# Strassen mixing on one Trainium2 core: operands made two slots ahead, the first sweep in fours, and u turned behind its exchange

## The chip, the cores and the metric

One Trainium2 chip, one of its cores. The metric is the device time of one launch in microseconds (us). The core's engines work side by side, each through its own instructions in program order: PE (matrix multiply; PEld is its weight load), DVE (vector), ACT (scalar, activation functions), POOL (GpSimd), and SP, which here only issues transfers between the device memory (DRAM) and the on-chip buffer. Matrix results land in banks of PSUM.

## The reference

All numbers are fp32. x is 2048 x 512; the caches hold 32 heads of 128.

```
xn  = layernorm(x)
s   = concat_h( softmax(q_h k_h^T / sqrt(128)) v_h ) @ wo      # last 512 cached keys, q = xn @ wq
z   = gelu(xn @ w_in)                                          # 2048 x 1376
z1, z2 = z[:, :688], layernorm(z[:, 688:])
g   = w_sp @ z2 + b_sp[:, None]                                # w_sp is 2048 x 2048: the "mixing"
out = x + s * silu((z1 * g) @ w_out)
```

The kernel keeps fp32 accuracy on a faster matmul type (fp32r): each operand is split into a high part (a cast, on ACT) and a low part (the operand minus its high part, on DVE or POOL, the helper at line 59), and each product is three matmuls, high by high, high by low, low by high.

## The kernel before, in words

The program runs in four stages, one after the other on PE. Attention and z1 come first, up to 1451 us; the change leaves them as they are. Then **z2**: 16 tiles of 128 rows in the order 8 to 15, 0 to 7 (`ZO`), two 344-column products each; ACT applies gelu while it reads PSUM (L775), DVE takes statistics (L776, L782), POOL makes the reciprocal root for a pair of tiles (L74, L75), DVE normalises both tiles (L788), and `z_split` (L792 on ACT, the low part on POOL) makes the operand of the first products.

Then the **mixing**, by one level of Strassen-Winograd. w_sp is cut in quarters a11, a12, a21, a22, and z2 in four quarters b11 to b22 (rows by columns). For each of 8 row blocks r (128 rows of the upper and 128 of the lower half) there are 7 products, P1 to P7. The 56 products are slots (`SLOTS`, `NS`): a sweep of P2 and P1 for all r, 16 slots, and then P6, P5, P7, P3, P4 for r = 0, r = 1 and so on; `first(r)` is the slot of P6. A slot is 24 matmuls of 128 x 344. Its weights are an operand made by `prep`: a cast on ACT (L832) and a rest on DVE (L59, 128 x 1024), for P4 on POOL. P5, P7, P6 and P3 need sums of quarters of w_sp (s1 = a21 + a22, a11 - a21, s1 - that, a12 - that), four `a_sum` instructions per row block (L820), the last of them on POOL. Their moving side is z2's quarters or the differences T1 to T4 of them (`t_diff`, L867; split at L876).

What sets the order: no planner, a table of events. `on(t, f, ...)` puts a call at slot t; `step(t)` first makes the operand of slot t + 2 and then runs the events of slot t. The main loop emits, for each slot, the products, then the eviction of the slot before, then the step. Every engine's queue is this program order; an instruction waits for its inputs and for its buffer to come free. Most buffers of the mixing are the eight 8 KB ones of `x8`: rows of w_sp, operands, s1, small blocks.

Evictions (`evict_1` for the sweep, `evict_2`) add products in DVE: U = P1 is stored to DRAM in the sweep and loaded again by `load_2` in the slot before P6 of its row block, with the first half of u and the rest of z1; P6's eviction (L995) adds U. A finished row block of u = z1 * g is turned in 32 x 32 squares on DVE (L986, 768 columns) and stored; the last stage loads it in another order, which completes its transpose.

Last the **out-projection**: 16 tiles of 17 matmuls of 128 x 512 (`project`), each with a load of turned u, s and x (`load_p`), a split (`split_u`: L1056 on ACT, L59 128 x 640 on DVE) and `finish_out` (silu on ACT, L1072; two DVE instructions, L1073, L1074; the store).

Of the kernel before, what the change touches and what calls it, by code (L numbers as in the profile page):

```python
# [17 lines left out]
P = 128  # L18
# [7 lines left out]
ZW = 352  # L26
# [14 lines left out]
def mixer_kernel(ctx: ExitStack, tc: tile.TileContext, x, wh, w_in, w_sp, b_sp, w_out, out):  # L41
# [715 lines left out]
    zp = ctx.enter_context(tc.tile_pool(name="zp", bufs=1, side="right", reuse_waits="tile"))  # L757
    bz = tuple(zp.tile([P, NT, ZW], F32R, name=f"bz_{a}") for a in "hl")
    zr_stack = ExitStack()
    zrp = zr_stack.enter_context(tc.tile_pool(name="zrp", bufs=1, side="right", reuse_waits="tile"))  # L760
    zr = zrp.tile([P, NT, 2, NB], F32, name="zr")
    p1_dram = dram.tile([P, RP, NB], F32, name="p1_dram")
    u0_dram = dram.tile([P, RP, NB], F32, name="u0_dram")
    uD = dram.tile([NT, P, NF * P], F32, name="u_dram")
# [7 lines left out]
    def z_gelu(i, n):  # L772
        if n == 2:
            zst[i] = stats.tile([P, 2, 6], F32, name="stz")
        nc.scalar.activation(zr[:, i, n - 2], zps[i, n][:, :NB], AF.Gelu_apprx_tanh)  # L775
        nc.vector.bn_stats(zst[i][:, n - 2, :], zr[:, i, n - 2])  # L776

    def z_norm(pos):
        g, j = divmod(pos, 2)
        if j == 0:  # L780
            zmv[g] = stats.tile([P, 2, 2], F32, name="mvz")
        nc.vector.bn_aggr(zmv[g][:, j, :], zst[ZO[pos]])  # L782
        if j == 1:
            r = stats.tile([P, 2], F32, name="rz_r")
            rsqrt(zmv[g][:, :, 1], r, 2, stats.tile([P, 2], F32, name="rz_t"))
            for k in range(2):
                t = zr[:, ZO[pos - 1 + k]].rearrange("p n f -> p (n f)")
                nc.vector.tensor_scalar(t, t, zmv[g][:, k, 0:1], r[:, k:k + 1], op0=OP.subtract, op1=OP.mult)  # L788

    def z_split(i, engine):  # L790
        hi, lo = (t[:, i, :NB] for t in bz)
        nc.scalar.copy(hi, zr[:, i, 0])  # L792
        rest(engine, lo, zr[:, i, 0], hi)


    SLOTS = [(r, k) for r in range(RP) for k in ("P2", "P1")] \
# [7 lines left out]
    rows, s1, ops, tt, t2, bank = {}, {}, {}, {}, {}, {}  # L804
# [5 lines left out]
    def a_blocks(r):  # L810
        HW = RP * P
        return rows["a", r][:, :HW], rows["a", r][:, HW:], rows["b", r][:, :HW], rows["b", r][:, HW:]

    def a_sum(r, k, engine):
        a11, a12, a21, a22 = a_blocks(r)
        if k == 0:
            s1[r] = x8([P, RP * P], F32)
        to, x0, x1, op = ((s1[r], a21, a22, OP.add), (a21, a11, a21, OP.subtract),
                          (a11, s1[r], a11, OP.subtract), (a12, a12, a11, OP.subtract))[k]
        engine.tensor_tensor(to, x0, x1, op=op)  # L820

    def prep(n, engine):
        r, k = SLOTS[n]
        HW = RP * P
        if k in ("P2", "P1"):
            src = rows["s", r][:, HW:] if k == "P2" else rows["s", r][:, :HW]
# [8 lines left out]
    def operand(k, c):  # L835
        if k in ("P1", "P4"):
            return tuple(t[:, c, :NB] for t in bz)
        if k in ("P2", "P3"):
            return tuple(t[:, RP + c, :NB] for t in bz)
        return tuple(t[:, c, :NB] for t in tt[k])  # L840

    def products(n):
# [3 lines left out]
        if first_of:  # L846
            bank[r, name] = pp.tile([P, 512], F32, name=name)
        ps = bank[r, name][:, :NB]
        op = ops.pop(n)
        for c in range(RP):  # L850
            rh, rl = operand(k, c)
# [5 lines left out]
    def pair(j):  # L857
        return slice(2 * j, 2 * j + 2), slice(RP + 2 * j, RP + 2 * j + 2)

    def t_diff(j, k):  # L860
        c, d = pair(j)
        b11, b12, b21, b22 = zr[:, c, 0], zr[:, c, 1], zr[:, d, 0], zr[:, d, 1]
        if k == "T2":
            t2[j] = t2_tile[:, j % 2, :, :NB]
        to, x0, x1 = {"T1": (b11, b12, b11), "T3": (b12, b22, b12), "T2": (t2.get(j), b22, b11),
                      "T4": (b21, b21, t2.get(j))}[k]
        nc.vector.tensor_tensor(to, x0, x1, op=OP.subtract)  # L867

    def t_split_z(j, k, engine):
        c, d = pair(j)  # L870
        src = {"T2": t2.get(j), "T1": zr[:, c, 0], "T3": zr[:, c, 1], "B22": zr[:, d, 1], "T4": zr[:, d, 0]}[k]
        if k in ("B22", "T4"):
            hi, lo = (t[:, d if k == "B22" else c, :NB] for t in bz)
        else:
            hi, lo = (t[:, c, :NB] for t in tt[{"T2": "P6", "T1": "P5", "T3": "P7"}[k]])
# [9 lines left out]
    for r in range(RP):  # L885
        on(2 * r - 6 if r else -8, load_rows, ("s", r), r)
        on(first(r) - 7, load_rows, ("b", r), r + RP)
        on(first(r) - 6, load_rows, ("a", r), r)
        for k, (d, e) in enumerate(((-4, V), (-3, V), (-3, V), (-2, G))):
            on(first(r) + d, a_sum, r, k, e)  # L890
    for j in range(4):
        on(-4 + 2 * j, t_diff, j, "T1")
        on(-4 + 2 * j, t_diff, j, "T3")
        on(3 * j + 1, t_diff, j, "T2")
        on(3 * j + 1, t_split_z, j, "T2", V)
        on(3 * j + 2, t_diff, j, "T4")
        on(3 * j + 2, t_split_z, j, "T1", V)
        on(3 * j + 3, t_split_z, j, "T3", V)
        on(15, t_split_z, j, "B22", G)
        on(16, t_split_z, j, "T4", V)  # L900

    def step(t):
        if 0 <= t + 2 < NS and t + 2 > 1:
# [24 lines left out]
    M = FH - (NF - 1) * P  # L928
    pp = ctx.enter_context(tc.tile_pool(name="pp2", bufs=2, space=PSUM, reuse_waits="tile"))
    tpool = {}  # L930
    for k in ("P7", "P5", "P6"):
        tpool[k] = ExitStack() if k == "P6" else ctx
        pool = tpool[k].enter_context(tc.tile_pool(name=f"tp{k}", bufs=1, reuse_waits="tile"))
# [214 lines left out]
```

## Time and profile before

| | us |
|---|---|
| median of 3 runs (lowest to highest) | 1826.93 (1826.82 to 1831.71) |
| the profiled execution: its time, its span | 1824.3, 1822.5 |
| PE busy in the span | 1778.2 (98%) |
| DVE, ACT, POOL busy | 1516.3, 1174.9, 1287.3 |
| z2 stage, 1451.0 to 1508.4: PE busy | 56.89 of 57.4 |
| mixing, 1508.4 to 1750.6: PE busy | 66.84 of 71.6 up to 1580.0, then 152.97 of 170.6 |
| out-projection, 1750.6 to 1818.0: PE busy | 64.05 of 67.4 |

How to read it: a share over the whole span says little here, since attention fills 80% of it at a busy PE. The stages that the change touches are read one by one: how long PE was in each, how long it would take at the pace of an undisturbed stretch, and which wait ended last before each gap. In rows of a timeline the bracket at the end is the idle time of the engine before the instruction and what ended it.

### The profile page before, as it was taken

How to read it: one execution, taken by the hardware profiler on the slowest of the kernel's cores; microseconds unless marked ns; L12 is line 12 of the kernel's file. 1: busy time of each engine (PE TensorE's matmuls, PEld its weight loads, DVE VectorE, ACT ScalarE, POOL GpSimd, SP SyncE). 2: the span in 40 equal slices, each digit the busy share in tenths (PEclk: the TensorE clock that was granted, in tenths of full speed). 3: DMA queues.
4: the chain of work that ended last, by engine and by line, in shares of the span. 5: the costliest groups of instructions: out<-in, count | busy, mean ns of one | idle time of the engine just before them, and what ended most of it. 6: DMA issues, size and time to landing. Idle time of an engine off the chain costs nothing.

```text
span 1822.5 us, 28703 instructions
## 1 busy us (share of the span) xinstructions
PE 1778.2 (98%) x8460; PEld 1516.2 (83%) x8460; DVE 1516.3 (83%) x2468; ACT 1174.9 (64%) x2632; POOL 1287.3 (71%) x1203
## 2 busy tenths in 40 slices
PE   8999999999999999999999999999999999799998
PEld 7888888888888887888888888888888998798987
DVE  5689988899999888888888888888888467788865
ACT  4777777767777776677777777777776434533333
POOL 2798898898998987788888888888887241233220
PEclk9999999999999999999999999999999999999999
DMA  5688897988988989787777877877777724445488
GB/s 186 196 231 237 252 263 224 264 240 246 268 241 237 266 252 281 257 243 228 223 217 230 223 218 230 232 220 233 223 232 233 255 73 151 167 166 182 150 259 245
DMA packets 182526, 408.89 MB, mean 224 GB/s; under 512 B 24448, under 2 KB 61568, under 8 KB 162144
## 3 DMA queue, kind: packets, MB, share of 16 engines
q1 hardware_dynamic: 175456, 398.59, 73.4%
q10 hardware_dynamic: 6912, 8.46, 1.3%
q8 instruction: 66, 1.08, 0.2%
q14 instruction: 92, 0.75, 0.1%
HBM read 237.02 MB, written 169.93 MB: 223 GB/s over the span
## 4 chain that ended last, share of the span: by engine, by line
PE 74%; DVE 12%; DMA 7%; ACT 3%; issue 2%; SPq 1%; POOL 1%; ACTq 0%; DVEq 0%; POOLq 0%
PE ps_a L450 15%; PE ps L67 12%; PE ps L65 12%; PE ps L66 12%; PE ps_a L517 6%; PE ps_a L515 6%; PE ps_a L516 6%; DVE x L820 2%; DMA U<-p_dram 2%; DVE x L59 2%; PE ps_a L65 2%; PE ps_a L66 2%; PE ps_a L67 2%; DMA x<-u_dram 1%; DMA p_dram<-pL 1%
## 5 line engine op out<-in xcount | busy, mean ns | idle before, releaser
L59 POOL TENSOR_TENSOR pT_l<-pL,pT_h 128x512 fp32r<-128x512 f32 x507 | 657.4, 1300 | 186.0 <-ACT pT_h L507 181.1
L479 ACT ACTIVATE prob<-ps,nm 128x512 f32<-128x512 f32 x512 | 354.0, 691 | 340.0 <-DVE nm L477 332.3
L539 DVE SCALAR_TENSOR_TENSOR sacc<-ps,sums,sacc 128x512 f32<-128x512 f32 x496 | 369.7, 746 | 128.1 <-PE ps L67 122.5
L450 PE MATMUL ps_a<-x,x 128*128 128x512 f32 x1302 | 376.4, 389 | 4.3 <-DMA x<-x_dram 3.3
L488 DVE STREAM_TRANSPOSE pL<-prob 128x512 f32<-128x512 f32 x512 | 358.6, 700 | 2.7 <-ACT prob L479 2.7
L477 DVE TENSOR_REDUCE nm<-ps 128x1 f32<-128x512 f32 x512 | 340.0, 664 | 6.6 <-PE ps L67 6.5
L507 ACT CAST pT_h<-pL 128x512 fp32r<-128x512 f32 x512 | 318.5, 622 | 18.4 <-DMA x<-x_dram 6.7
L450 PEld LDWEIGHTS ps_a<-x,x 128*128 128x128 f32 x1302 | 244.5, 188 | 56.3 <-DMA x<-x_dram 4.1
L59 POOL TENSOR_TENSOR wl<-raw,wh 128x512 fp32r<-128x512 f32 x186 | 241.7, 1299 | 13.4 <-ACT wh L144 13.4
L517 PE MATMUL ps_a<-pT_l,wh 128*128 128x512 f32 x512 | 200.4, 391 | 1.6 <-POOL pT_l L59 1.5
L65 PE MATMUL ps<-wh,qT_h 128*128 128x512 f32 x512 | 199.9, 390 | 0.6 <-DVE sacc L539 0.6
L67 PE MATMUL ps<-wh,qT_l 128*128 128x512 f32 x512 | 199.9, 390 | 0.3
L515 PE MATMUL ps_a<-pT_h,wh 128*128 128x512 f32 x512 | 200.0, 391 | 0.0
L65 PE MATMUL ps<-wh,oT_h 128*128 128x512 f32 x512 | 199.7, 390 | 0.0
L67 PE MATMUL ps<-wh,oT_l 128*128 128x512 f32 x512 | 199.5, 390 | 0.0
L66 PE MATMUL ps<-wl,qT_h 128*128 128x512 f32 x512 | 199.5, 390 | 0.0
L516 PE MATMUL ps_a<-pT_h,wl 128*128 128x512 f32 x512 | 199.5, 390 | 0.0
L66 PE MATMUL ps<-wl,oT_h 128*128 128x512 f32 x512 | 199.4, 390 | 0.0
L59 POOL TENSOR_TENSOR x<-wq,x 128x256 fp32r<-128x256 f32 x186 | 138.5, 745 | 1.5 <-ACT x L432 1.5
L144 ACT CAST wh<-raw 128x512 fp32r<-128x512 f32 x188 | 117.9, 627 | 2.0 <-issue 1.1
L517 PEld LDWEIGHTS ps_a<-pT_l,wh 128*128 128x128 f32 x512 | 96.2, 188 | 24.4 <-POOL pT_l L59 4.7
L67 PEld LDWEIGHTS ps<-wh,qT_l 128*128 128x128 f32 x512 | 96.3, 188 | 22.0 <-DVE qT_l L59 2.0
(213 smaller groups left out, 3375.5 us busy)
## 6 DMA issues: line engine op xcount, KB each, us to landing
p_dram<-pL SPq DMA_DIRECT2D x128, 1024.0 KB, 4.8
pL<-p_dram SPq DMA_DIRECT2D x256, 192.0 KB, 4.0
raw<-wh SPq DMA_DIRECT2D x188, 256.0 KB, 6.3
pL<-p_dram SPq DMA_DIRECT2D x256, 128.0 KB, 4.0
x<-w_sp SPq DMA_DIRECT2D x24, 1024.0 KB, 5.1
pL<-p_dram SPq DMA_DIRECT2D x256, 64.0 KB, 4.0
wq<-wh SPq DMA_DIRECT2D x62, 256.0 KB, 5.6
x_dram<-rawx SPq DMA_DIRECT2D x32, 256.0 KB, 6.0
```

Source lines behind the costliest of these rows:

```text
L59: engine.tensor_tensor(lo, whole, hi.bitcast(F32), op=OP.subtract)
L65: nc.tensor.matmul(ps, lh, rh, start=first, stop=False)
L66: nc.tensor.matmul(ps, lh, rl, start=False, stop=False)
L67: nc.tensor.matmul(ps, ll, rh, start=False, stop=last)
L450: nc.tensor.matmul(qps[g, bank], wt["q", g, k][a][:, c * P:(c + 1) * P], X[g * 2 // H][ORDER[k]][:, b, c], start=first, stop=r == 5, skip_ ...
L477: nc.vector.tensor_reduce(nm, ps, axis=AX.X, op=OP.max, negate=True)
L479: nc.scalar.activation(prob[t], ps, AF.Exp, bias=nm, accum_out=sums[b][:, j:j + 1])
L488: nc.vector.transpose(pL[b][:, :, j * P:j * P + P].rearrange("p a (c q) -> p a c q", q=Q), prob.pop(t).rearrange("p (a c q) -> p a c q", a ...
L507: nc.scalar.copy(h, p)
L515: nc.tensor.matmul(pps[b], vh, ph, start=c == 0, stop=False)
L517: nc.tensor.matmul(pps[b], vh, pl, start=False, stop=c == 3)
L539: nc.vector.scalar_tensor_tensor(at, ps, rs, at, op0=OP.mult, op1=OP.add)
```

## The change

- z2 and its differences are kept in blocks of one size from one pool (`br`, 20 blocks, and `bl`, 5) instead of large fixed tiles; blocks are handed out anew as they come free. For the last eight tiles of z2 the normalisation is done by ACT (an Identity activation with scale and bias, L805), with two one-column POOL instructions per pair ahead of it (L804).
- The sweep goes P2 of r = 0 to 3, P1 of r = 0 to 3, P2 of r = 4 to 7, P1 of r = 4 to 7. Its rows of w_sp come as halves for two r at a time (`load_halves`).
- s1 has a buffer of its own; all four a_sums are on DVE; the T differences and splits have other slots; half of the last splits go to POOL.
- U of r = 0 stays on chip; for the others it is loaded four slots ahead of P6. z1 is loaded in thirds at f - 3 to f - 1, gelu at f to f + 2, and u is stored unturned in halves at f + 4 to f + 6. P5's eviction is one DVE add instead of an ACT copy; P7's eviction goes to a PSUM bank. The two-bank pools become 2, 4 and 2 banks (ps_a, ps_c, ps_f).
- In the out-projection tiles are loaded four ahead and split two ahead; `split_u` turns u after the load (two DVE transposes); the last add is on POOL; x is loaded apart from u and s. w_out, reordered on the host, is loaded at slot 43, and the first two tiles are split at the last two slots of the mixing.
- In the main loop the eviction and the step come ahead of the slot's products in program order.

```diff
+    def hilo(k, j, pool=None):
+        if pool is not None:
+            HL[k, j] = blk(pool)
+        return tuple(HL[k, j][:, a, :, :NB] for a in range(2))
...
     def z_norm(pos):
...
+                if pos < RP:
+                    nc.vector.tensor_scalar(t, t, mean, rs, op0=OP.subtract, op1=OP.mult)
+                else:
+                    nc.gpsimd.tensor_scalar(tmp[:, k:k + 1], mean, rs, -1.0, op0=OP.mult, op1=OP.mult)
+                    nc.scalar.activation(t, t, AF.Identity, bias=tmp[:, k:k + 1], scale=rs)
...
-    SLOTS = [(r, k) for r in range(RP) for k in ("P2", "P1")] \
+    SLOTS = [(r, k) for g in range(0, RP, 4) for k in ("P2", "P1") for r in range(g, g + 4)] \
         + [(r, k) for r in range(RP) for k in ("P6", "P5", "P7", "P3", "P4")]
...
-    for r in range(RP):
-        on(2 * r - 6 if r else -8, load_rows, ("s", r), r)
-        on(first(r) - 7, load_rows, ("b", r), r + RP)
-        on(first(r) - 6, load_rows, ("a", r), r)
-        for k, (d, e) in enumerate(((-4, V), (-3, V), (-3, V), (-2, G))):
-            on(first(r) + d, a_sum, r, k, e)
-    for j in range(4):
-        on(-4 + 2 * j, t_diff, j, "T1")
-        on(-4 + 2 * j, t_diff, j, "T3")
-        on(3 * j + 1, t_diff, j, "T2")
-        on(3 * j + 1, t_split_z, j, "T2", V)
-        on(3 * j + 2, t_diff, j, "T4")
-        on(3 * j + 2, t_split_z, j, "T1", V)
-        on(3 * j + 3, t_split_z, j, "T3", V)
-        on(15, t_split_z, j, "B22", G)
-        on(16, t_split_z, j, "T4", V)
...
+    for j in range(4):
+        on((-8, -4, 4, 6)[j], load_halves, "P2", j)
+        on((0, 2, 8, 10)[j], load_halves, "P1", j)
+        on((-5, -3, -1, 0)[j], t_diff, j, "T1")
+        on((-5, -3, -1, 0)[j], t_diff, j, "T3")
+        on((-4, -2, 0, 1)[j], t_diff, j, "T2")
+        on((-4, -2, 0, 1)[j], t_diff, j, "T4")
+        on((0, 0, 1, 2)[j], t_split, j, "T2", V)
+        on((2, 3, 3, 4)[j], t_split, j, "T1", V)
+        on((4, 5, 6, 7)[j], t_split, j, "T3", V)
+        on((12, 12, 13, 14)[j], t_split, j, "B22", V)
+        on((16, 16, 16, 17)[j], t_split, j, "T4", G if j % 2 else V)
+    for r in range(RP):
+        f = first(r)
+        on(f - 7 if r else 6, load_rows, ("b", r), r + RP)
+        on(f - 6 if r else 7, load_rows, ("a", r), r)
+        for k, d in enumerate((-4, -3, -3, -1) if r else (-7, -6, -6, -5)):
+            on(f + d, a_sum, r, k)
...
+    def load_U(r):
+        us[r, "U"] = sm.tile([P, NB], F32, name="p1", bufs=3)
         nc.sync.dma_start(us[r, "U"], p1_dram[:, r])
...
         elif k == "P5":
-            us[r, "p5"] = pm.tile([P, NB], F32, name="p5", bufs=2)
-            nc.scalar.copy(us[r, "p5"], c)
+            us[r, "up5"] = sm.tile([P, NB], F32, name="z1", bufs=4)
+            nc.vector.tensor_tensor(us[r, "up5"], c, U, op=OP.add)
         elif k == "P7":
-            u3 = pm.tile([P, NB], F32, name="u3", bufs=2)
-            nc.vector.tensor_tensor(u3, a, U, op=OP.add)
-            nc.vector.tensor_tensor(u3, u3, us[r, "p5"], op=OP.add)
-            gate(r + RP, 1, u3)
+            g = pp.tile([P, 512], F32, name="ps_f")[:, :NB]
+            nc.vector.tensor_tensor(g, a, us[r, "up5"], op=OP.add)
+            gate(r + RP, 1, g)
...
-            send_u(r)
...
         if r:
-            on(first(r) - 1, load_2, r)
-        on(first(r) + 1, gelu_2, r)
-        on(first(r) + 2, gelu_2, r + RP)
+            on(f - 4, load_U, r)
+        for k, (i, n) in enumerate(((r + RP, 1), (r, 1), (r + RP, 0))):
+            on(f - 3 + k, load_z1, i, n, k)
+            on(f + k, gelu_z1, i, n)
+            on(f + 4 + k, store_u, i, n)
...
     def split_u(i):
...
+        nc.vector.transpose(to[:, :, :NF - 1], uL[:, :, :NF - 1])
+        nc.vector.transpose(to[:64, :, NF - 1], uL[:64, :, NF - 1])
+        nc.scalar.copy(hi[:, :e], whole[:, :e])
+        nc.scalar.copy(hi[:64, e:], whole[:64, e:])
+        rest(nc.vector, lo[:, :e], whole[:, :e], hi[:, :e])
+        rest(nc.vector, hi[64:, e:], whole[64:, e:], hi[64:, e:])
...
     for t in range(NS):
-        if t == SWEEP + 1:
-            zr_stack.close()
-            pm = ctx.enter_context(tc.tile_pool(name="pm", bufs=1, side="right", reuse_waits="tile"))
-            load_2(0)
-        products(t)
...
         step(t)
+        products(t)
     evict_2(RP - 1, "P4")
...
     for n, i in enumerate(PO):
-        if n == 0:
-            split_u(i)
-        if n + 3 < NT:
-            load_p(PO[n + 3])
+        if n + 2 < NT:
+            split_u(PO[n + 2])
...
         project(i)
-        split_u(PO[n + 1])
-        finish_out(i)
+        finish_out(i, nc.gpsimd)
+        if n + 2 < NT:
+            load_xp(PO[n + 2])
+        if n + 4 < NT:
+            load_p(PO[n + 4])
+        send_out(i)
```

Three places in the instruction order, of before and of the change. The first is ACT at the last tiles of z2 (zr and, in the change, b are blocks of z2; bz_h its high part; x with a number is a row buffer or an operand in an 8 KB buffer; rz_r the reciprocal root). Before:

```order
L775 ACTIVATE zr<-ps_a 128x344 x2
L792 CAST bz_h<-zr 128x344
L832 CAST x_18683<-x_18528 128x1024
L775 ACTIVATE zr<-ps_a 128x344 x2
L792 CAST bz_h<-zr 128x344
L775 ACTIVATE zr<-ps_a 128x344 x2
L792 CAST bz_h<-zr 128x344
L775 ACTIVATE zr<-ps_a 128x344 x2
L792 CAST bz_h<-zr 128x344 x3
L832 CAST x_18862<-x_18686 128x1024
```

The change:

```order
L856 CAST x_18696<-x_18530 128x1024
L787 ACTIVATE b<-ps_a 128x344 x2
L805 ACTIVATE b<-b,rz_t,rz_r 128x2x344 x2
L812 CAST b<-b 128x344
L787 ACTIVATE b<-ps_a 128x344 x2
L812 CAST b<-b 128x344
L787 ACTIVATE b<-ps_a 128x344 x2
L805 ACTIVATE b<-b,rz_t,rz_r 128x2x344 x2
L812 CAST b<-b 128x344 x3
L856 CAST x_18849<-x_18701 128x1024
```

The gelus of z2's last tiles (L787) now stand behind normalisations (L805) in ACT's queue; these were DVE's before.

The second place is DVE from there to the operands of the third and fourth products (stz, mvz: statistics; L867 and L886 are T differences; L59 the rests). Before:

```order
L867 TENSOR_TENSOR zr<-zr 128x2x344 x2
L776 BN_STATS stz<-zr 128x6 x2
L782 BN_AGGR mvz<-stz 128x2
L788 TENSOR_SCALAR zr<-zr,mvz,rz_r 128x688 x2
L59 TENSOR_TENSOR bz_l<-zr,bz_h 128x344
L59 TENSOR_TENSOR x_18862<-x_18686,x_18862 128x1024
L867 TENSOR_TENSOR zr<-zr 128x2x344 x2
L59 TENSOR_TENSOR x_18895<-x_18686,x_18895 128x1024
```

The change:

```order
L886 TENSOR_TENSOR b<-b 128x2x344 x2
L788 BN_STATS stz<-b 128x6 x2
L794 BN_AGGR mvz<-stz 128x2
L886 TENSOR_TENSOR b<-b 128x2x344 x2
L788 BN_STATS stz<-b 128x6 x2
L794 BN_AGGR mvz<-stz 128x2
L886 TENSOR_TENSOR b<-b 128x2x344 x2
L59 TENSOR_TENSOR b<-b 128x344
L59 TENSOR_TENSOR x_18849<-x_18701,x_18849 128x1024
L59 TENSOR_TENSOR b<-b 128x2x344 x2
L886 TENSOR_TENSOR b<-b 128x2x344 x4
L59 TENSOR_TENSOR x_18889<-x_18701,x_18889 128x1024
```

Two differences now stand before each of the last two tiles' statistics, two more before the rest of the third product's operand, and two splits and four differences between it and the fourth's.

The third place is DVE in one row block, from P6's eviction to P4's operand. Before (u, U, p are row blocks of the output and partial sums):

```order
L995 TENSOR_TENSOR u_19661<-ps_a,U 128x344
L59 TENSOR_TENSOR x_19663<-x_19392,x_19663 128x1024
L820 TENSOR_TENSOR x_19666<-x_19557 128x1024
L820 TENSOR_TENSOR x_19557<-x_19592,x_19557 128x1024
L820 TENSOR_TENSOR x_19592<-x_19666,x_19592 128x1024
L1001 TENSOR_TENSOR u_19725<-ps_a,U 128x344
L1002 TENSOR_TENSOR u_19725<-u_19725,p_19693 128x344
L977 MEMSET u 128x80
```

The change:

```order
L988 TENSOR_TENSOR b<-ps_a,p_19499 128x344
L59 TENSOR_TENSOR x_19660<-x_19414,x_19660 128x1024
L845 TENSOR_TENSOR s_19663<-x_19566 128x1024
L991 TENSOR_TENSOR z_19694<-ps_c,p_19499 128x344
L845 TENSOR_TENSOR x_19566<-x_19599,x_19566 128x1024
L845 TENSOR_TENSOR x_19599<-s_19663,x_19599 128x1024
L994 TENSOR_TENSOR ps_f<-ps_a,z_19694 128x344
L965 SCALAR_TENSOR_TENSOR b<-ps_f,bsp,b 128x344
L59 TENSOR_TENSOR x_19731<-x_19599,x_19731 128x1024
```

P5's eviction (L991) is now a DVE instruction between the sums, and the padding and turning of u are gone from the block.

More of the change, by code (lines that the diff above doesn't have):

```diff
@@ L25 @@
 NF = (FH + P - 1) // P
-ZW = 352
+ZW = 384
 EPS = 1e-5
@@ L846, in products @@
         if first_of:
-            bank[r, name] = pp.tile([P, 512], F32, name=name)
+            bank[r, name] = pp.tile([P, 512], F32, name=name, bufs=2 if name == "ps_a" else 4)
         ps = bank[r, name][:, :NB]
@@ L971, in gelu_2 @@
-    def gelu_2(i):
-        nc.scalar.activation(us[i, "z"], us[i, "z"], AF.Gelu_apprx_tanh)
-    def gate(i, n, c):
-        if i >= RP and n:
-            us[i, "u"] = pm.tile([P, NF * P], F32, name="u", bufs=4)
-            nc.vector.memset(us[i, "u"][:, FH:], 0.0)
-        u, z1 = us[i, "u"], us[i, "z"]
-        at = 0 if i < RP else n * NB
-        for lo, hi, to in ((0, NB, n * NB), (NB - M, NB, FH - M + 64))[:1 + n]:
-            nc.vector.scalar_tensor_tensor(u[:, to:to + hi - lo], c[:, lo:hi], bsp[:, i:i + 1],
-                                           z1[:, at + lo:at + hi], op0=OP.add, op1=OP.mult)
@@ L1033, in split_wo @@
[L1033 to L1038 removed]
+            on(f - 4, load_U, r)
[3 more added lines that the diff above has]
+            on(f + 4 + k, store_u, i, n)
+    wo, uT, up = {}, {}, {}
```

258 lines of the change are left out of this document (131 added, 127 removed).

## The prediction

> **What bounds the kernel now.** I read by stage: the windows first, then what PE waited for, then the chain behind the longest wait. The windows of the last four stages (columns: PE, PEld, DVE, ACT and POOL busy, the granted clock, the DMA share, GB/s):
>
> ```profile
> 1451.00:1508.40 57.40, 56.89 (x372) 56.61 (x370) 33.92 (x63) 22.55 (x49) 23.77 (x29) 1.00 0.31 111
> 1508.40:1580.00 71.60, 66.84 (x405) 63.70 (x406) 53.45 (x64) 34.04 (x51) 7.82 (x7) 1.00 0.50 171
> 1580.00:1750.60 170.60, 152.97 (x941) 150.83 (x940) 145.08 (x166) 56.94 (x73) 54.75 (x25) 0.97 0.50 166
> 1750.60:1818.00 67.40, 64.05 (x288) 50.84 (x286) 41.30 (x67) 22.81 (x32) 0.93 (x1) 1.00 0.92 270
> ```
>
> z2 is full on PE. The mixing isn't, and from 1580 on DVE is as long as the stage: 145.08 of 170.6. The price of the lost time comes from PE's own timeline: the first product, the next two slots' starts, the gaps, the first projection matmul, a tile's start and the next tile's, the last matmul:
>
> ```profile
> 1508.43 0.43 PE L853 MATMUL ps_c<-bz_h,x 128*128 128x344 f32 x1 [0.55 <-ACT zr L775]
> 1512.33 0.32 PE L853 MATMUL ps_a<-bz_h,x 128*128 128x344 f32 x1
> 1516.11 0.32 PE L853 MATMUL ps_c<-bz_h,x 128*128 128x344 f32 x1
> 1591.67 0.62 PE L853 MATMUL ps_a<-tP_h,x 128*128 128x344 f32 x1 [7.24 <-DVE u L995]
> 1676.83 0.40 PE L853 MATMUL ps_a<-tP_h,x 128*128 128x344 f32 x1 [2.38 <-DVE u L995]
> 1750.63 0.40 PE L65 MATMUL ps_f<-woh,x 128*128 128x512 f32 x1
> 1753.74 0.50 PE L67 MATMUL ps_f<-woh,x 128*128 128x512 f32 x1 [2.48 <-DVE x L59]
> 1757.31 0.40 PE L65 MATMUL ps_f<-woh,x 128*128 128x512 f32 x1
> 1761.19 0.40 PE L65 MATMUL ps_f<-woh,x 128*128 128x512 f32 x1
> 1818.35 0.28 PE L1068 MATMUL ps_f<-wol,x 128*128 128x256 f32 x1
> ```
>
> An undisturbed slot takes 1516.11 - 1512.33 = 3.78 us. 56 of them are 211.7; the mixing took 1750.63 - 1508.43 = 242.2. **30.5 us are lost in the mixing.** An undisturbed tile of the projection takes 3.88 (1761.19 - 1757.31); 15 of them and a last one in halves (34 matmuls, 0.12 apart) are 62.2, against 1818.63 - 1750.63 = 68.0: **5.8 are lost there.** Together 36.3; more than that, with all else as it is, this change can't win. PE's waits over the last 380 us, in total, times and longest, name one owner:
>
> ```profile
> PE ps_a L853 <- DVE u L995: 17.6, 7, 7.2
> PE ps_c L853 <- DVE x L59: 2.9, 5, 0.7
> PE ps_f L67 <- DVE x L59: 2.5, 1, 2.5
> ```
>
> L995 is P6's eviction. Behind the longest gap and in the next row block the chain that ended last reads (start, length):
>
> ```profile
> 1588.58 2.34 DMA U<-p_dram
> 1606.39 5.89 DMA U<-p_dram
> 1616.45 3.30 DVE x L820
> ```
>
> U is asked for one slot before it is added, and takes longer than a slot to land; every DVE instruction behind L995 then waits with it, the sums for the next block among them. The groups of the last 320 us (count, busy, mean ns) give the prices:
>
> ```profile
> L59 DVE TENSOR_TENSOR x<-x,x 128x1024 fp32r<-128x1024 f32 x46 | 55.5, 1209 | 12.2 <-ACT x L832 11.9
> L820 DVE TENSOR_TENSOR x<-x,x 128x1024 f32<-128x1024 f32 x16 | 34.1, 2132 | 0.5
> L820 DVE TENSOR_TENSOR x<-x 128x1024 f32<-128x1024 f32 x8 | 9.7, 1217 | 0.0
> L1002 DVE TENSOR_TENSOR u<-u,p 128x344 f32<-128x344 f32 x8 | 17.9, 2241 | 0.8
> L986 DVE STREAM_TRANSPOSE uB<-u 128x768 f32<-128x768 f32 x16 | 15.7, 979 | 0.6
> L867 DVE TENSOR_TENSOR zr<-zr 128x688 f32<-128x688 f32 x6 | 5.2, 864 | 0.1
> L943 DVE TENSOR_TENSOR ps_c<-ps_c,x 128x344 f32<-128x344 f32 x8 | 4.1, 517 | 2.0 <-ACT x L941 2.0
> L944 DVE SCALAR_TENSOR_TENSOR x<-ps_c,bsp,x 128x344 f32<-128x344 f32 x8 | 4.6, 576 | 0.3
> L59 POOL TENSOR_TENSOR x<-x,x 128x1024 fp32r<-128x1024 f32 x8 | 24.8, 3102 | 104.9 <-ACT x L832 61.2 <-DVE x L820 43.7
> ```
>
> **The change part by part.** *What it removes.* Per row block DVE loses L1002 (2.24, long because POOL works beside it), both turns (2 x 0.98), the padding and two short pieces of the gate; it gains the fourth sum and P5's add. It then holds four rests (4 x 1.21), four sums (4 x 1.22, the price without POOL beside them), five adds (5 x 0.52) and three gates (3 x 0.58): 4.84 + 4.88 + 2.60 + 1.74 = 14.1 us, against five slots of 18.9. POOL keeps only P4's rest, at most 3.1: even if it stopped DVE throughout, 17.2 is under 18.9. U is asked for four slots (15 us) ahead, against a landing of 5.9. The first row block's U doesn't travel, and its sums are in the sweep. So I take nearly all 30.5 as removed, with **1.0** left for short waits like the 0.7 ones of L59 (bounds 0 and 8: L59's waits of 2.9, and a gap such as 2.4 in two blocks more). ACT was busy for a third of that stage (56.94 of 170.6) and gains no more than it loses, and what SP issues more (stores in halves, loads in thirds) lies in a stage whose DMA share is 0.50.
>
> *What it adds: the handover from z2 to the mixing.* Here ACT and DVE get work into queues on which the first products wait. Rows of before: a gelu, two differences beside POOL, a tile's two statistics, POOL's root, and the nearest rows for L804 and L805:
>
> ```profile
> 1493.20 0.46 ACT L775 ACTIVATE zr<-ps_a 128x344 f32<-128x344 f32 x1 [1.38 <-PE ps_a L67]
> 1498.38 4.06 DVE L867 TENSOR_TENSOR zr<-zr 128x688 f32<-128x688 f32 x2
> 1506.38 0.92 DVE L776 BATCH_NORM_STATS2 stz<-zr 128x6 f32<-128x344 f32 x2
> 1503.92 0.71 POOL L75 TENSOR_TENSOR rz_r<-rz_t,power 128x2 f32<-128x2 f32 x1
> 1495.52 0.93 POOL L59 TENSOR_TENSOR bz_l<-zr,bz_h 128x344 fp32r<-128x344 f32 x1
> L285 POOL TENSOR_SCALAR rs_t<-mv,rs_r x8: 266/267/268, 161.7 to 533.8; 128x1 f32<-128x1 f32 x8
> L288 ACT ACTIVATE rawx<-rawx,rs_t,rs_r x8: 814/822/836, 168.5 to 566.2; 128x512 f32<-128x512 f32 x8
> ```
>
> An Identity pass over 688 columns isn't in the trace: at least the 0.82 of 512 columns, at most 0.82 x 688 / 512 = 1.10; I take 0.95, 1.9 for a pair. Statistics of a tile with their aggregate are 1.13, the root with both L804 instructions 1.0 + 2 x 0.27 = 1.53, a pair of differences 1.73. I number z2's tiles by position, 0 to 15, in the new order.
>
> Position 11's second gelu ends at 1493.66. Statistics 0.7, root 1.53: 1495.9. Two L805 (positions 10 and 11): 1497.8. The cast of position 9 stands behind them, 0.47, then its low part on POOL, 0.93: 1499.2. The first pair's T1 and T3 overwrite what that low part reads, so they wait: 1500.9. Position 12's statistics: 1502.1. T2, T4: 1503.8. Position 13's statistics: 1504.9. Root: 1506.5. Two L805: 1508.4. A cast, two gelus, a cast, two gelus: 2.8, **1511.1**, when the first product starts, 2.7 after the old 1508.43.
>
> The third product: the cast of position 11 and its low part follow those L805: 1509.8; T1, T3 of the second pair: 1511.5; statistics of 14: 1512.7; T2, T4: 1514.4; statistics of 15: 1515.5; root: 1517.0; two L805: 1518.9; the cast and low part of 13: 1520.3; T1, T3 of the third pair: 1522.0; the last z2 rest 0.8, the operand's rest 1.21: 1524.1. PE would be there at 1511.1 + 7.6 = 1518.7: **5.4 lost**. The fourth: two splits (1.73, taken as long as differences, which have as many columns), four differences (3.46) and its rest (1.21) are 6.4, a slot is 3.78: **2.6 lost**. The fifth: one split, two differences and its rest, 3.8: nothing. From there a slot's queue is under a slot. Sum 2.7 + 5.4 + 2.6 = 10.7. Bounds: 0, if the waits for the low parts resolve earlier than the queue order makes them; and 10.7 + 2 x 2.3 = 15.3, if two pairs of differences meet a POOL rest as at 1498.38 (4.06 for 1.73).
>
> *The clock.* After gaps PE ran slower:
>
> ```profile
> 1592.00:1604.00 12.00, 12.00 (x67) 12.00 (x67) 11.78 (x12) 4.45 (x6) 4.81 (x2) 0.85 0.33 114
> 1676.00:1688.00 12.00, 11.17 (x61) 11.20 (x62) 11.64 (x11) 4.45 (x6) 5.84 (x2) 0.86 0.43 158
> ```
>
> 61 matmuls at 3.78 / 24 are 9.6 and took 11.17: 1.6 us for the gap of 2.38; the one of 2.48 in the projection cost nothing (1.00). So each of the three new gaps costs 0 to 1.6; I take **1.6** once, for the longest. [...]
>
> *The projection.* The change splits two tiles ahead of the product, the first two inside the mixing, so the 2.48 gap goes. But DVE turns each tile after its load:
>
> ```profile
> x<-u_dram SPq DMA_DIRECT2D x56, 96.0 KB, 4.3
> L1056 ACT CAST x<-x 128x768 fp32r<-128x768 f32 x16 | 13.4, 835 | 30.0 <-DMA x<-u_dram 30.0
> ```
>
> Two turns are 0.98 x 640 / 768 = 0.8 and the small one; from the moment a product frees a buffer, four issues (1.8), landing (4.3), turn, cast, rest (0.8 each) are 8.5, for two tiles and a bit (7.8 to 8.2): 0.2 to 0.3 a tile over 12 tiles, say **2.5** (bounds 0; or 12, below).
>
> *Sum.* Lost after: 1.0 + 10.7 + 1.6 + 2.5 = 15.8; gain 36.3 - 15.8 = 20.5. Span 1822.5 - 20.5 = 1802.0; with the 1.8 around the profiled span, 1803.8. The profiled run (1824.3) lies 2.6 under the median 1826.93, so a median lies between 1803.8 and 1806.4: **1805**.
>
> **The rivals.** *The handover is hidden.* that DVE was idle for 23 of 57 us in z2 (33.92 busy) speaks for it; the waits for the low parts against. Then 10.7 and 1.6 shrink to about 3: gain 30, 1796.
>
> *The projection is bound by its loads.* A DMA share of 0.92 and 270 GB/s in that window speak for it, that PE waited only 2.9 there before, against. If u lands in 6 us instead of 4.3 the loop is 10.2 for 8.2, 1.0 a tile, 12 in all in place of 2.5: 1814 to 1815.
>
> *The change doesn't bring the operands earlier.* Rows and operands still share the eight 8 KB buffers, and SP's stores of u, which wait for gates, stand ahead of row loads. If a row load comes a slot late in each block, the 2.4 gap with its 1.6 of clock returns in six blocks: 24 lost for 1: 1828. For it: the gaps of L995 came seven times. Against: its owner there was U, not the rows.
>
> *DVE becomes the bound: slower.* One mechanism: POOL's instructions stop DVE's as L867 was stopped at 1498.38. It decides from 18.9 - 14.1 = 4.8 us of stopping per block; with the a_sum gone from POOL 3.1 are there. Were the stop twice that and the sums at 2.13 as in their row (14.1 + 4 x 0.9 + 6.2 = 23.9), each block would be 5 longer: 40 more, less the gain of 20: 1846; half of it, 1826 to 1836. [...]
>
> **How the numbers follow.** Forecast 0.58, hidden handover 0.12, loads 0.14, operands late 0.08, DVE bound 0.08. The forecast's own range takes the bounds of the handover and the clock: 1805 - 9 to 1805 + 8, 1796 to 1813. The range of 8 in 10 takes in the hidden handover and the loads: 1794 to 1818. About 0.3%, 5.5 us, is what a measurement can tell from no change. Faster than 1821.4: all of the first three but a rest, 0.83; within 0.3%: 0.10, mostly operands late; slower: 0.07.
>
> **What would show it.** No wait of PE on P6's eviction over 1 us; three gaps, before the first, third and fourth product, of about 3, 5 and 3 us, owned by ACT's gelu and DVE's L59; DVE at 14 of 19 us per block; the clock below 1.00 only behind these gaps; the mixing near 1511 to 1733; 16 tiles in 65. It would be wrong if PE waits recur once per row block, or once per tile in the projection.

## The result, and the profile after

| | before | changed |
|---|---|---|
| median of 4 runs, us (lowest to highest) | 1826.88 (1824.80 to 1831.71) | 1808.64 (1808.24 to 1812.95) |
| profiled execution: time, span | 1824.3, 1822.5 | 1808.75, 1807.0 |
| first product of the mixing starts | 1508.43 | 1513.06 |
| mixing | 242.2 | 222.6 |
| out-projection, first to last matmul | 68.0 | 67.2 |

The ratio is 0.990 (95% interval 0.988 to 0.993): faster, by 18.2 us in the medians and 15.5 in the spans of the profiled executions. Forecast were 1805 and a gain of 20.5 in the span.

The windows of the change, with the columns of the table of windows before:

```profile
1451.00:1508.00 57.00, 57.00 (x373) 56.80 (x371) 27.86 (x54) 22.80 (x46) 22.95 (x31) 1.00 0.27 93
1508.00:1520.00 12.00, 7.02 (x28) 6.94 (x28) 6.07 (x10) 3.96 (x9) 4.86 (x9) 0.72 0.36 117
1520.00:1532.00 12.00, 8.79 (x41) 8.21 (x40) 8.68 (x10) 8.46 (x12) 1.99 (x3) 0.74 0.00 0
1532.00:1544.00 12.00, 12.00 (x76) 12.00 (x76) 11.97 (x15) 8.00 (x13) 0.00 (x0) 0.98 0.62 190
1603.00:1735.00 132.00, 132.00 (x838) 132.00 (x837) 104.23 (x111) 44.75 (x60) 26.64 (x13) 1.00 0.54 172
1735.00:1803.00 68.00, 65.48 (x295) 51.90 (x293) 44.20 (x80) 23.03 (x48) 19.37 (x15) 1.00 0.79 231
```

From 1603 to 1735, where seven row blocks run, PE has no gap at all, and DVE is busy for 104 of 132 us (114.55 there before). Most of what is lost now lies in the 24 us behind z2, at a mean clock of 0.72 to 0.74. PE's waits from 1440 on, and then the timeline of PE, with its gaps in the mixing and the first matmul of the projection:

```profile
PE ps_c L872 <- ACT b L787: 5.0, 1, 5.0
PE ps_c L872 <- DVE x L59: 2.8, 1, 2.8
PE ps_f L65 <- DVE x L1078: 2.4, 3, 1.2
PE ps_c L872 <- DVE z L991: 1.4, 1, 1.4
PE ps_c L872 <- ACT x L856: 0.4, 1, 0.4
```

```profile
1513.06 10.46 PE L872 MATMUL ps_c<-b,x 128*128 128x344 f32 x48 [4.98 <-ACT b L787]
1523.93 0.59 PE L872 MATMUL ps_c<-b,x 128*128 128x344 f32 x2 [0.41 <-ACT x L856]
1527.32 2.95 PE L872 MATMUL ps_c<-b,x 128*128 128x344 f32 x9 [2.80 <-DVE x L59]
1595.42 4.02 PE L872 MATMUL ps_c<-b,x 128*128 128x344 f32 x24 [1.41 <-DVE z L991]
1735.66 0.39 PE L65 MATMUL ps_f<-b,x 128*128 128x512 f32 x1
```

P6's eviction (L988 now) is gone from the waits. The account: the start is 4.6 us later than before; the mixing's 222.6 are 10.9 over 56 undisturbed slots (211.7), of which 4.6 are gaps and some 6 the slow clock (the first two products take 10.46 for 7.57); the projection is 5.0 over 62.2; the stretch behind the last matmul is 0.2 longer. 36.3 - 4.6 - 10.9 - 5.0 - 0.2 = 15.6, against 15.5 between the rounded spans.

The handover on DVE, POOL and ACT shows why:

```profile
1500.18 2.40 DVE L886 TENSOR_TENSOR b<-b 128x688 f32<-128x688 f32 x2 [5.54 <-POOL b L59]
1503.59 2.88 DVE L886 TENSOR_TENSOR b<-b 128x688 f32<-128x688 f32 x2
1512.27 2.38 DVE L886 TENSOR_TENSOR b<-b 128x688 f32<-128x688 f32 x2 [4.71 <-POOL b L59]
```

```profile
1509.06 1.81 ACT L805 ACTIVATE b<-b,rz_t,rz_r 128x688 f32<-128x688 f32 x2 [7.22 <-POOL rz_t L804]
1512.20 0.81 ACT L787 ACTIVATE b<-ps_a 128x344 f32<-128x344 f32 x2
```

T1 and T3 of a pair wait for the low part of its second tile (POOL L59, 1500.18 and 1512.27, 12.1 us apart); ACT sits idle for 7.2 us ahead of a normalisation, with the gelus of z2's last four products queued behind it; the last gelu ends at 1513.0, and PE starts.

The rests of the third and the fourth product, on DVE, end at 1527.3 and 1533.4, the first of them 6.6 us after two products at full clock would have (1513.06 + 7.57):

```profile
1526.05 1.22 DVE L59 TENSOR_TENSOR x<-x,x 128x1024 fp32r<-128x1024 f32 x1
1532.14 1.22 DVE L59 TENSOR_TENSOR x<-x,x 128x1024 fp32r<-128x1024 f32 x1
```

### The profile page after: what moved, and what is told of

It is laid out like the page before. It is cut to its first block, busy times and chain, and to the rows that moved or that the text cites. A ratio compares the mean times of both kernels' runs of the same rounds, so it can differ in the third digit from the quotient of the medians.

```text
span 1807.0 us, 28702 instructions
## 1 busy us (share of the span) xinstructions
PE 1775.9 (98%) x8460; PEld 1517.7 (84%) x8460; DVE 1495.8 (83%) x2439; ACT 1179.1 (65%) x2656; POOL 1282.5 (71%) x1215
## 4 chain that ended last, share of the span: by engine, by line
PE 88%; DVE 5%; ACT 2%; issue 2%; DMA 2%; POOL 1%; SPq 1%; ACTq 0%; DVEq 0%; POOLq 0%
PE ps_a L450 15%; PE ps L67 12%; PE ps L65 12%; PE ps L66 12%; PE ps_a L872 6%; PE ps_a L517 6%; PE ps_a L515 6%; PE ps_a L516 6%; PE ps_c L872 5%; PE ps_a L65 2%; PE ps_a L67 2%; PE ps_a L66 2%; PE ps_f L65 1%; DVE nm L477 1%; PE ps_f L66 1%
## 5 line engine op out<-in xcount | busy, mean ns | idle before, releaser
L59 POOL TENSOR_TENSOR pT_l<-pL,pT_h 128x512 fp32r<-128x512 f32 x507 | 655.9, 1297 | 186.5 <-ACT pT_h L507 170.6
L507 ACT CAST pT_h<-pL 128x512 fp32r<-128x512 f32 x512 | 318.5, 622 | 20.5 <-DMA pL<-p_dram 10.0
L59 POOL TENSOR_TENSOR wl<-raw,wh 128x512 fp32r<-128x512 f32 x186 | 241.1, 1296 | 11.9 <-ACT wh L144 11.9
L59 POOL TENSOR_TENSOR x<-wq,x 128x256 fp32r<-128x256 f32 x186 | 137.9, 742 | 1.5 <-ACT x L432 1.5
L872 PE MATMUL ps_a<-b,x 128*128 128x344 f32 x768 | 124.0, 320 | 0.0
L872 PEld LDWEIGHTS ps_a<-b,x 128*128 128x128 f32 x768 | 121.6, 188 | 0.0
```

Of the source, the lines that this page charges most:

```text
L59: engine.tensor_tensor(lo, whole, hi.bitcast(F32), op=OP.subtract)
L507: nc.scalar.copy(h, p)
L872: nc.tensor.matmul(ps, a, b, start=first_of and c == 0 and m == 0, stop=c == RP - 1 and m == 2, skip_group_check=True)
```

## The experiments

Each ran on one chip with runs of the kernel before; the change's median of 1808.6 comes from another such group. A few tenths of a per cent between groups are therefore not read; the gaps in the profiles are.

### What freed the row blocks

U late again in the change:

```diff
-            on(f - 4, load_U, r)
+            on(f - 1, load_U, r)
```

> The change with one thing undone: U of row blocks 1 to 7 is asked for one slot ahead of P6 again, not four. If the early U is what freed the row blocks, P6's or P5's eviction waits for U again in seven blocks, 1.5 to 2.5 us each, some with a slower clock behind: 10 to 20 us longer than the change, 1819 to 1829. If it was the DVE time taken out of the blocks (turns, padding, the sum beside POOL), U still arrives in time and the run stays within 3 us of the change's 1808.6.

1808.0 us (0.991 of before, 0.989 to 0.992), and no gap on an eviction but the 1.4 of the first block. The early place of U isn't needed in the changed kernel; which of its other parts makes up for it, this run alone doesn't tell. The other direction, U early in the kernel before:

```diff
     def load_2(r):
-        us[r, "U"] = pm.tile([P, NB], F32, name="U", bufs=2)
-        nc.sync.dma_start(us[r, "U"], p1_dram[:, r])
...
+            on(first(r) - 4, load_U, r)
             on(first(r) - 1, load_2, r)
```

> The kernel before with one thing added: U is asked for four slots ahead of P6 instead of one (the other loads stay). If the late U was the cause, the 10.4 us of gaps on P6's eviction in row blocks 1 to 7 go with the slower clock behind one of them: 10 to 14 us less than before, 1813 to 1817; the first block's gap of 7.2 stays. If DVE itself is too full there (145 of 171 us), the gaps move to other DVE instructions and it gains 3 at most: 1824 or more.

1811.5 us (0.993; 0.991 to 0.995), 13.2 under the kernel before in its group. Its waits (the eviction is line 997 here), in total, times and longest:

```profile
PE ps_a L853 <- DVE u L997: 7.2, 1, 7.2
```

On the eviction one gap is left, that of the first block; DVE is as busy as before (113.22 of 132 us from 1603 on) and isn't in the way. So in the other seven blocks the late U was the cause, and asking for it early is enough; in the changed kernel, what else was changed is enough. What removed the 7.2 of the first block (its U stays on chip, its sums are in the sweep) wasn't tried by itself; neither run touches it. Why one slot's notice suffices in the change is read from SP's queue. Before, in the fourth row block: SP's waits from 1603 to 1735, then its transfers, then the eviction:

```profile
SPq L988 <- DVE uB L986: 65.6, 11, 17.7
```

```profile
1647.85 0.32 SPq L988 DMA_DIRECT2D u_dram<-uB  x1
1648.26 0.38 SPq L808 DMA_DIRECT2D x<-w_sp  x1
1648.69 0.47 SPq L962 DMA_DIRECT2D U<-p_dram  x1
1654.63 0.52 DVE L995 TENSOR_TENSOR u<-ps_a,U 128x344 f32<-128x344 f32 x1 [2.46 <-DMA U<-p_dram]
```

The load of U stands behind the store of the block before, which waits for its turn on DVE (L986, 1646.84 and 0.98 long). U is issued 5.9 us ahead of the add, about its landing time, and 3.5 ahead of when DVE was free for the add (1654.63 - 2.46). In the run with U late in the change (its L981 and L988) a store of u stands right ahead of the load too, but it waits for no turn, only for a gate in the middle of its block (L965, done at 1652.94), and 9.7 us remain:

```profile
1652.97 0.32 SPq L968 DMA_DIRECT2D u_dram<-b  x1
1653.34 0.42 SPq L981 DMA_DIRECT2D p<-p_dram  x1
1663.04 0.52 DVE L988 TENSOR_TENSOR b<-ps_a,p 128x344 f32<-128x344 f32 x1 [1.51 <-PE ps_a L872]
```

A run with nothing moved but the store, which would test this reading alone, wasn't made.

### The handover: operands early, other banks

The operands of the third and fourth product made during z2's last two tiles:

```diff
-        if 1 < t + 2 < NS:
+        if 3 < t + 2 < NS:
...
+        if t in (-2, -1):
+            prep(t + 4, nc.gpsimd)
```

> The change with the operands of the third and fourth product made at the last two tiles of z2 (rest on POOL) instead of behind z2's last normalisations. If the third product waits because its rest stands in DVE's queue behind the T differences, the gaps of 0.4 and 2.8 us before and in it go, and with them the slow clock behind the second: 3 to 6 us less than the change, 1802.5 to 1805.5; the first gap of 5.0 and the slow first two products stay. If the two rests on POOL hold up the last low parts and normalisations instead, the gap before the first product grows and the sum stays within 1.5 of 1808.6.

1811.1 us (0.993; 0.992 to 0.995): no gain. The first gap grew from 5.0 to 6.0, and the others moved to the fifth product, before it (its cast) and in it (its rest):

```profile
1532.95 0.58 PE L872 MATMUL ps_a<-b,x 128*128 128x344 f32 x2 [2.57 <-ACT x L856]
1537.37 4.84 PE L872 MATMUL ps_a<-b,x 128*128 128x344 f32 x19 [3.84 <-DVE x L59]
```

With the sums on other banks too (ps_c in a pool of its own, opened behind the one of ps_a and ps_f):

> The run before this one (early operands for the third and fourth product), and the sums ps_c in PSUM banks that z2's last gelus don't read. If the gap of 5.0 before the first product is only the wait for the last gelu's bank, the first product starts at about 1508.2 without a gap, the first four run at full clock to about 1523.3, and the fifth waits at most 3 for the last low part of z2: 9 to 14 us less than the change, 1795 to 1800. If the first product has another wait behind the bank (its z2 blocks or operands), the gap stays and it ends with e3_prep_early.

1811.1 us (0.992; 0.990 to 0.995). The first product did start at 1508.17 without a gap, so the 5.0 us are only the wait for the last gelu's bank. But the time came back in four gaps before 1539. Whatever the first products wait for, the operands behind them come at the pace of z2's normalisations, and these were not touched.

### The handover: two circles

The split of a tile moved ahead of the present pair's normalisation:

```diff
-        z_norm(pos)
         if pos > 1:
             z_split(ZO[pos - 2], nc.gpsimd)
+        z_norm(pos)
```

> The change with two calls swapped in the loop over z2's tiles: the split of the tile two positions back is emitted ahead of the statistics, root and normalisation of the present pair, not behind them. If the handover is the circle read in the trace (T1, T3 of a pair wait for a low part that stands behind the next pair's normalisation, whose statistics stand behind T1, T3; some 12 us a pair against 7.4 of z2's products), it opens: the first product starts by 1509.5 with a gap under 1.5, the third waits under 3, the fourth about 2.6, no stretch below a clock of 0.9 longer than 6 us: 5 to 9 us less than the change, 1799.5 to 1803.5. If the normalisations on ACT are slow by themselves, the first gap stays at 4 or more and the time within 1.5 of 1808.

1805.6 us (0.989; 0.987 to 0.992). The wait for low parts is shorter, yet the first gap is 4.88, and the normalisation ahead of it starts 1.3 us behind z2's last product (1.0 in the change); on DVE, on ACT and on PE:

```profile
1497.12 1.78 DVE L886 TENSOR_TENSOR b<-b 128x688 f32<-128x688 f32 x2 [1.81 <-POOL b L59]
1503.16 4.33 DVE L886 TENSOR_TENSOR b<-b 128x688 f32<-128x688 f32 x2
```

```profile
1499.87 1.81 ACT L805 ACTIVATE b<-b,rz_t,rz_r 128x688 f32<-128x688 f32 x2 [4.99 <-POOL rz_t L804]
1511.19 1.81 ACT L805 ACTIVATE b<-b,rz_t,rz_r 128x688 f32<-128x688 f32 x2 [6.43 <-POOL rz_t L804]
```

```profile
1514.81 9.36 PE L872 MATMUL ps_c<-b,x 128*128 128x344 f32 x48 [4.88 <-ACT b L787]
```

Normalisations are still 11.3 us apart, for 7.4 of z2's products. The time lies between the two that were expected, and my reading of one circle fell: there is a second, of nearly the same length. A gelu stands behind the pair's normalisation in ACT's queue, its statistics and two differences follow on DVE (4.33 beside POOL here), then the second tile's statistics, POOL's root, and the next normalisation. With the early operands on top of the swap:

> The swap and the early operands of the third and fourth product together. By the circle the first four products now have all they need and the fifth waits under 1 for the last low part of z2: no gap over 1.5 before 1540, clock 1.00: 9 to 12 us less than the change, 1796 to 1799. If the two rests on POOL cost what they cost alone (the gaps moved to the fifth and sixth product), it stays within 1.5 of the swap alone.

1808.3 us (0.990; 0.988 to 0.993): a first gap of 5.8 and one of 3.7 in the fifth product. Missed too, since it rested on the first circle alone.

Two runs cut the second circle in two ways. The normalisations back on DVE:

```diff
-                if pos < RP:
+                if pos < NT:
                     nc.vector.tensor_scalar(t, t, mean, rs, op0=OP.subtract, op1=OP.mult)
```

> The change with the normalisations of z2's last eight tiles back on DVE, the rest as in the change. After the swap the circle is read as: gelu, statistics, two differences, statistics, root, the pair's normalisation on ACT, and the next gelu behind it in ACT's queue. If that is it, gelus no longer stand behind normalisations: the gap of 5.0 before the first product falls to 0.5 to 1, the products start near 1508.6 at full clock; the third still waits for its rest behind the differences. 2 to 6 us less than the change: 1802.5 to 1806.5. If DVE is what the circle lacks (four normalisation pairs of 1.8 us more in its queue), the first gap stays at 4 or more and the time is equal or up to 4 longer.

1801.5 us (0.987; 0.986 to 0.989). The first gap is nearly gone, as the circle has it; the third product still waits:

```profile
1510.81 7.84 PE L872 MATMUL ps_c<-b,x 128*128 128x344 f32 x48 [0.55 <-ACT b L787]
1520.59 0.58 PE L872 MATMUL ps_c<-b,x 128*128 128x344 f32 x2 [1.94 <-ACT x L856]
1522.93 1.51 PE L872 MATMUL ps_c<-b,x 128*128 128x344 f32 x4 [1.76 <-DVE x L59]
1520.00:1532.00 12.00, 9.65 (x44) 9.37 (x45) 11.90 (x14) 6.62 (x9) 0.58 (x1) 0.72 0.15 39
```

And the normalisations left on ACT, but emitted one tile later:

```diff
-                    nc.scalar.activation(t, t, AF.Identity, bias=tmp[:, k:k + 1], scale=rs)
+                    apply.append((t, tmp[:, k:k + 1], rs))
...
+        z_apply()
         z_norm(pos)
```

(`z_apply` runs what is in the list; it is called once more behind the last tile.)

> The change with each pair's normalisation emitted one tile later on ACT, behind the next tile's gelus instead of ahead of them; statistics, root and all else stay. If the circle runs through ACT's queue order, it opens: first gap under 1, start by 1509, clock 1.00 over the first two products: 4 to 8 us less than the change, 1800.5 to 1804.5, unless the third product's gap grows by as much. If the differences' wait for low parts alone sets the pace, the first gap stays at 4 or more, and the time within 1.5 of 1808.

1803.2 us (0.988; 0.987 to 0.990), the first gap 2.3, not under 1, and full clock behind it:

```profile
1511.24 7.83 PE L879 MATMUL ps_c<-b,x 128*128 128x344 f32 x48 [2.31 <-ACT b L787]
```

Same engine, same work, another place in its queue: that place, not ACT's speed, made most of the first gap. From z2's last matmul to the first of the projection, which leaves out what varies ahead of it, the change takes 227.6 us, the swap 225.7, the early operands 230.0, and both of these last runs 221.1: 6.5 less than the change.

The normalisations themselves still come slower than z2's products. With them on DVE:

```profile
1497.97 1.78 DVE L802 TENSOR_SCALAR b<-b,mvz,rz_r 128x688 f32<-128x688 f32 x2 [1.14 <-POOL rz_r L75]
1508.19 1.79 DVE L802 TENSOR_SCALAR b<-b,mvz,rz_r 128x688 f32<-128x688 f32 x2 [1.14 <-POOL rz_r L75]
```

They are 10.2 us apart there (10.0 in the other run), still more than the 7.4 of z2's products. By these rows, what the two runs took away is above all the wait of the last gelus, and with them of PE's banks, for this chain (all of it on DVE, about half when deferred); the operands made behind it still wait.

### The projection

Six banks in turn instead of two:

```diff
-        us[i, "f"] = pp.tile([P, D], F32, name="ps_f")
+        us[i, "f"] = pp.tile([P, D], F32, name="ps_f") if PO.index(i) % 3 == 0 else pp.tile([P, D], F32, name="ps_c", bufs=4)
```

> The change with the projection's sums in six PSUM banks in turn instead of two. If PE's gaps there (2.4 us, on DVE's multiply L1078) are only the wait for a bank, they go: 2 to 3 us less than the change, 1805.5 to 1806.5. If the operands of the next tiles are late themselves (u lands late, so the turn and the split are late), the gaps come back under ACT's cast or DVE's rest and the time stays within 1 of 1808.

1805.9 us (0.989; 0.987 to 0.991), and PE's list of waits from 1730 on is empty; the projection takes 63.9 us for 67.2. The gaps were the wait for a bank, which DVE's multiply (L1078) frees late because it stands behind a turn (L1057) that waits for u. In the change, on DVE and then on PE:

```profile
1769.06 0.85 DVE L1057 STREAM_TRANSPOSE x<-x 128x640 f32<-128x640 f32 x1 [1.97 <-DMA x<-u_dram]
1771.92 0.69 DVE L1078 TENSOR_TENSOR x<-ps_f,x 128x512 f32<-128x512 f32 x1
1772.66 0.50 PE L65 MATMUL ps_f<-b,x 128*128 128x512 f32 x1 [1.21 <-DVE x L1078]
```

The operands themselves, split two tiles ahead, were in time. The three changes together:

> The swap, the early operands and the six banks together. The sum of the three if each works: 1794 to 1797; the same as the swap with the early operands if the banks bring nothing.

1806.7 us (0.990; 0.987 to 0.992), a miss by some 10 us: the projection has no gaps, but the handover is as it was with the swap and the early operands (gaps of 5.8 and 3.8).

### A version that beats both

The deferred normalisation, the early operands with their rests on DVE, the later differences and six banks:

```diff
-        on((-5, -3, -1, 0)[j], t_diff, j, "T1")
+        on((-5, -3, 1, 3)[j], t_diff, j, "T1")
...
-        on((-4, -2, 0, 1)[j], t_diff, j, "T2")
+        on((-4, -2, 2, 4)[j], t_diff, j, "T2")
...
-        on((0, 0, 1, 2)[j], t_split, j, "T2", V)
-        on((2, 3, 3, 4)[j], t_split, j, "T1", V)
-        on((4, 5, 6, 7)[j], t_split, j, "T3", V)
+        on((0, 1, 3, 5)[j], t_split, j, "T2", V)
+        on((5, 6, 7, 8)[j], t_split, j, "T1", V)
+        on((8, 9, 10, 11)[j], t_split, j, "T3", V)
```

(T3 moves with T1, T4 with T2.)

> The deferred normalisation, the operands of the third and fourth product made at z2's last two tiles with their rests on DVE, the differences and splits of the third and fourth pair spread over two to four slots more, and six PSUM banks in the projection. If queue order is all that is left in the handover and DVE's load there (12.0 of 12 us busy from 1532 to 1544) is the second limit, neither leaves a gap over 1.5: the mixing takes 212 to 216 us from 1508.5: 1793 to 1798. If spreading doesn't help since the sum of DVE's work up to the sixth product is the limit, a gap of 3 to 5 stays near 1530 to 1537 and it ends at 1800 to 1805.

1797.5 us (0.985; 0.983 to 0.987). The gaps behind the first product are gone, but for the 1.4 of the first row block and 0.3 in the projection. The one before it is 3.25, where at most 1.5 was expected, and the clock behind it is slow. The four runs spread (1794.6, 1795.0, 1799.9, 1801.2; mean clock 0.998 in the first two, 0.997 and 0.994 in the others), and the profile is of the longest:

```profile
1513.92 10.31 PE L879 MATMUL ps_c<-b,x 128*128 128x344 f32 x47 [3.25 <-ACT b L787]
1508.00:1520.00 12.00, 8.75 (x40) 8.48 (x39) 8.25 (x14) 5.13 (x8) 5.50 (x9) 0.72 0.54 189
```

The same with the normalisations on DVE:

> The run before this one with the normalisations of z2's last eight tiles on DVE again instead of deferred on ACT (early operands of the third and fourth product with rests on DVE, spread differences, six banks as there). If the gap of 3.25 us before the first product and the slow clock behind it (0.72 from 1508 to 1520) are what is left of the handover, the first gap falls to about 0.6 at full clock, as with the normalisations on DVE alone: 2 to 6 us less than 1797.5, 1791.5 to 1795.5. If DVE's load becomes the limit, a gap of 2 to 5 comes before the third to sixth product and it ends at 1796 to 1800.

1793.8 us (0.982; 0.980 to 0.983), 14.8 under the change by the medians. Its waits from 1500 to the end:

```profile
PE ps_c L872 <- DVE z L993: 1.4, 1, 1.4
PE ps_c L872 <- ACT b L787: 1.4, 1, 1.4
```

```profile
1509.87 14.30 PE L872 MATMUL ps_c<-b,x 128*128 128x344 f32 x89 [1.41 <-ACT b L787]
1723.74 0.39 PE L65 MATMUL ps_f<-b,x 128*128 128x512 f32 x1
```

The mixing takes 213.9 us, 2.2 over its undisturbed slots.

## Why the prediction was right, and where its terms were off

The direction and the bound held: 36.3 us to win, some of it given back at the handover and in the projection. By its steps:

- *Row blocks, 1.0 left:* 1.4, one gap in the first block; none in the seven others. In the first, DVE's own splits of T4 (3.14 us for two beside POOL's) and the rest behind P6's eviction (2.27 for 1.21) delay P5's eviction. DVE's load was forecast as 14.1 per block; 104.23 in 132 us are 14.9 per 18.9: one of the four sums takes 3.42, not 1.22, beside POOL's rest of P4 (rows overlap at their ends, so the busy time rises by less). The reason given for U, "asked for one slot before it is added, and takes longer than a slot to land", was half of it: one slot of the table was enough in the change, where the load isn't held behind a store that waits for a late turn (by the rows of SP's queue). The forecast counted the early load and the missing turns as one change, without seeing that in seven blocks the late load alone was the cause.
- *The start, 2.7 late:* 4.6. The waits came in the order predicted, but differences took 2.4 to 2.9 for the 1.73 they were priced at, beside POOL. The Identity pass took 0.95 (a pair 1.81), as priced.
- *The wait of the differences for low parts* as the one cause fell as a sole cause: with it shortened, the gap stayed at 4.9. The gelu behind the normalisation, which stood in my chain as a line of the sum, is a circle by itself; taking the gelus out from behind it brought 5 to 7 us by the medians, 6.5 in the profiles.
- *Third and fourth product, 5.4 and 2.6:* the third's rest was done at 1527.3, forecast 1524.1; gaps of 0.4 and 2.8 in it, none before the fourth. The slow clock stretched the products over the wait: it was the same time, under another name.
- *The clock, 1.6 once:* some 6 of PE's time, but little of the kernel's. An estimate from the ends of the two rests (1527.3 and 1533.4) and 3.78 a slot: at full clock the third product would have lost 6.4 us and the fourth 2.3 in waits, and the fourth would have ended only some 0.2 us earlier than it did. So the two waits were forecast about right, and the clock's own price here was near nothing. That 8.0 + 1.6 forecast and 3.2 + 6.3 measured come to nearly the same sum is partly luck: I priced the clock by a gap of 2.4 and took it to come on top of the waits.
- *The projection, 2.5:* 5.0, the term mis-sized most. The sum took all of the 5.8 lost there before as gone and added the loop of loads. But only 2.9 of the 5.8 were waits that the change could remove; the rest were slower tiles, which it gave no reason to end. In the change 2.4 are gaps, about 1.2 are tiles of 3.96 for 3.88, and some 1.4 are late tiles that took longer still, which stays open. The loads were late, as the sum had it (the turn waits for them), but they reached PE through a bank and not through the operands: six banks removed the gaps with the same loads.
- *Sum:* 20.7 lost (0.2 of it behind the last matmul), forecast 15.8; the range's upper bounds covered it.

The hidden handover and DVE as the bound of the row blocks didn't occur. Late operands came once, at the handover. The projection wasn't bound by its loads at 1.0 a tile.

## What to carry to other kernels

An in-order queue turns one late instruction into a delay for what stands behind it, on a transfer queue (here the load of U behind a store, the add 2.46 us late) as on an engine (gelus behind a normalisation, a first gap of 4.98 us, 2.31 when that was deferred): read what stands ahead of the late one, not only when it was asked for. Where work for the next stage is slipped between the steps of a loop, follow the loop once round through all queues; if the way round is longer than the loop's own pace, every turn loses the difference, there can be two such ways, and what frees the busy engine's buffers should not stand behind them. A gap filled at one place reappears at the next late operand until the chain that makes the operands is shortened.

## What the runs showed of the hardware that was not expected

In these runs the clock behind gaps doesn't go by the length of one gap. With the deferred normalisation, one of 2.31 left it at 1.00 (48 matmuls in 7.83 us), and so did the next three, of 1.04, 1.10 and 2.04. With the normalisations on DVE, two of 1.94 and 1.76, which end 2.3 us apart, brought 0.72 over 12 us; in the version that defers, one of 3.25 brought 0.72. Read in finer windows, the 0.72 is a mean: the granted clock is one half for 6.8 us and full around it, in the change twice. The change, then the normalisations on DVE, then the version that defers:

```profile
1512.10:1518.90 6.80, 5.84 (x20) 5.84 (x21) 6.07 (x10) 0.91 (x3) 1.92 (x4) 0.50 0.21 78
1525.80:1532.60 6.80, 5.28 (x18) 5.28 (x19) 6.73 (x9) 2.75 (x4) 0.00 (x0) 0.50 0.00 0
1521.50:1528.30 6.80, 5.37 (x19) 5.37 (x20) 6.73 (x9) 3.71 (x5) 0.00 (x0) 0.50 0.00 0
1513.00:1519.80 6.80, 5.88 (x20) 5.88 (x21) 5.93 (x10) 2.18 (x5) 2.40 (x3) 0.50 0.45 172
```

In the kernel before it was at 0.50 for 6.8 us at the gap of 7.24 (from 1588.8) and for 3.4 behind that of 2.38 (from 1677.6). So one such stretch of 6.8 us costs PE an estimated 3.4 us at most, half of its length, and less where the next operand is late anyway. What sets such a stretch off, these runs leave open.

An undisturbed tile of the projection takes 3.96 us in every version with the change's blocks, 3.88 before, at the same granted clock and with as many matmuls. What makes them slower (the place of the weights, of w_out, or other traffic) wasn't tried.
